# Moving kv times wo and the column sums one to three gate/up pairs later, and spacing the 16 divisions 2.75 pairs apart

## The chip, the cores and the metric

The kernel runs on one core of one Trainium2 chip. The metric is the device time of one execution in microseconds (us). The span of a profile, from the first to the last instruction, is 1.7 to 1.9 us shorter than the time of its run. PE is the matmul engine, PEld its weight loads (they overlap the matmuls), DVE the Vector engine, ACT the Scalar engine, POOL the GpSimd engine, SP the engine that issues most of the DMA transfers. PSUM is the memory, in banks, into which the matmuls write.

## The reference

One block over 2048 tokens of width 512: layer norm, then the sum of the input, a linear attention with 32 heads of 16, and a SwiGLU feed-forward of width 1792. In bfloat16, cut to what matters:

```python
xn = layernorm(x)
q, k, v = heads(xn @ wqkv)                  # 32 heads of 16
pq, pk = phi(q), phi(k)                     # phi(t) = where(t > 0, t + 1, exp(t)) + 1e-6
kv  = einsum("bhsd,bhse->bhde", pk, v)
z   = einsum("bhsd->bhd", pk)               # the column sums of phi(k)
num = einsum("bhqd,bhde->bhqe", pq, kv)
den = einsum("bhqd,bhd->bhq", pq, z)[..., None] + 1e-6
A   = (num / den) @ wo
B   = (silu(xn @ w_gate) * (xn @ w_up)) @ w_down
return x + A + B
```

## The kernel before

The first stage (up to 48.5 us) normalises, projects and accumulates phi(k) transposed times xn in four PSUM banks. The second stage is a loop over 56 gate/up pairs: 4 chunks of 512 tokens times 14 slices of the width 1792. One pair is 4 gate and 4 up matmuls on PE. The attention work is threaded through this loop, and from the second chunk on an output tile of 128 tokens is put in after 4 of every 14 pairs; the last four tiles follow the loop. The parts that the change and the argument touch:

```python
def add(...):  # every operation is put on its engine's list in program order;
    ...        # semaphores are derived from what it reads and writes

def gb(j):
    return 4 + 2 * (j % 2)              # two pairs of PSUM banks, so pair j+2 reuses those of pair j

def hop(j):                             # hT = silu(gate) * up, DVE
    C, fc = j // NFC, j % NFC
    K.add("dve", lambda e: e.tensor_tensor(out=hT[:, C % 2, fc, :],
        in0=banks[gb(j) + 1][:, :], in1=sil[:, j % 2, :], op=ALU.mult), ...)

def z_add(half, i):                     # a "token sum": zacc += phi(k) of one tile of 128 tokens
    acc, key = zacc[:, half, :], ("zacc", half)
    t = NZP * half + i                  # NZP = 10: tiles 0..9 on POOL, tiles 10..15 on DVE
    ...
    K.add("dve" if half else "pool", lambda e: e.tensor_tensor(out=acc, in0=first, in1=pk[:, t, :], op=ALU.add), ...)

def kv_mask(): ...                      # DVE: kvT = bank 0 times a block mask
def m_mm(g): ...                        # PE: M = kvT times wo; ACT copies it out
def z_bf(): ...                         # DVE: zb (bf16) = zacc[0] + zacc[1]
def z_mm(): ...                         # PE: ones times zb, the column sums; ACT copies them out to zbc
def pz_mul(t): ...                      # POOL: pz = phi(q) times zbc
def divide(t): ...                      # DVE: reduce pz per head, + 1e-6, reciprocal, pq *= 1/den
                                        # then a DMA transposes pq into pk (the tile of phi(q) that PE reads)

for j in range(NGU):                    # 56 pairs
    C, fc = j // NFC, j % NFC
    if j == 2:
        gu(j, kv_fns(), ...)            # 16 small kv matmuls between those of the pair
    else:
        gu(j)
    if j == 0:
        hop(j)
    elif j == 1:
        hop(j); z_add(1, 1); z_add(1, 2)
    elif j == 2:
        hop(j); kv_mask(); z_add(1, 3)
    elif j == 3:
        hop(j); z_add(1, 4); z_add(1, 5); m_mm(0); m_mm(1)
    elif j == 4:
        hop(j); z_bf(); m_mm(2); m_mm(3)
    elif j == 5:
        hop(j); z_mm()
    else:
        if j % 2 == 0 and j // 2 - 3 < NT:
            pz_mul(j // 2 - 3)
        hop(j)
        if j % 2 == 1 and j // 2 - 3 < NT:
            divide(j // 2 - 3)
    if C >= 1 and fc in O_SLOT:         # an output tile
        otile(4 * (C - 1) + O_SLOT[fc])
```

(Statements of one pair are put on one line here; cuts are marked with dots.)

## Time and profile before

| | before |
|---|---|
| time, median of the first 3 runs | 215.41 us (215.18 to 215.76) |
| span of the profile | 213.3 us |
| PE busy | 208.3 us, 98% |
| DVE busy | 126.4 us, 59% |
| first gate matmul to first output tile (PE timeline, 48.50 to 84.60) | 36.10 us |
| first output tile to the end of the last matmul (84.60 to 210.85) | 126.25 us |

The head of the page of before, with busy time, share of the span and instructions of each engine:

```profile
span 213.3 us, 2668 instructions
PE 208.3 (98%) x991; PEld 95.5 (45%) x991; DVE 126.4 (59%) x217; ACT 69.8 (33%) x138; POOL 55.5 (26%) x81
```

PE at 98% does not say that it runs at its peak, because a record of a matmul covers its pipeline as well: a record of 512 columns lasts 0.38 us here, while the next one can start after 0.216 us. The chain of waits (start, length, what) shows the pace. These are pieces of the chain of before, with engine, tile and line after start and length:

```profile
60.39 0.68 DVE hT L395
61.07 0.61 DVE zb L419
61.73 0.39 PE pb L423
62.12 22.64 PE pb L382 x104
84.76 0.86 PE pb L461 x4
85.62 3.02 PE pb L465 x14
88.64 5.18 PE pb L382 x24
```

The last line gives 5.18 / 24 = 0.216 us for a matmul of 512 columns, each with a weight load of its own. The piece at 62.12 is slower: 104 matmuls in 22.64 us, 0.2177 each, 0.19 us more than at 0.2158. And the chain runs through DVE until 61.73: PE waits there for zb, the bf16 sum. From the table of waits of before (who waited for whom: us in total, times, longest), the two lines of PE in this stage and three lines of the weight loads:

```profile
PE pb L423 <- DVE zb L419: 0.6, 1, 0.6
PE pb L455 <- DVE kvT L413: 0.2, 1, 0.2
...
PEld pb L382 <- DVE hT L395: 1.1, 3, 0.4
PEld pb L423 <- DVE zb L419: 1.1, 1, 1.1
PEld pb L455 <- DVE kvT L413: 0.7, 1, 0.7
```

L423 is the column-sum matmul, L455 kv times wo, L382 gate and up. These waits understate the loss, since a matmul's record reaches beyond the moment at which the next could start; the starts in PE's timeline against a pace of 0.2158 us are the better measure:

```profile
55.44 1.03 PE L382 MATMUL pb<-xnT,wu 128*128 128x512 bf16 x4
56.65 0.61 PE L455 MATMUL pb<-wo,kvT 128*128 128x512 bf16 x2 [0.18 <-DVE kvT L413]
...
60.11 1.03 PE L382 MATMUL pb<-xnT,wu 128*128 128x512 bf16 x4
61.73 0.39 PE L423 MATMUL pb<-zb,ones 128*128 128x512 bf16 x1 [0.59 <-DVE zb L419]
```

Four matmuls after 55.44 is 56.30, and kv times wo starts at 56.65; four after 60.11 is 60.97, and the column-sum matmul starts at 61.73. The DVE timeline of before (start, length) shows what DVE did at the time:

```profile
53.86 1.53 DVE L332 TENSOR_TENSOR zacc<-zacc,pk 128x512 f32<-128x512 f32 x1
55.31 0.68 DVE L395 TENSOR_TENSOR hT<-pb,sil 128x512 bf16<-128x512 f32 x1
55.91 0.68 DVE L413 TENSOR_TENSOR kvT<-pb,maskt 128x512 bf16<-128x512 f32 x1
56.51 1.67 DVE L332 TENSOR_TENSOR zacc<-zacc,pk 128x512 f32<-128x512 f32 x1
58.11 0.68 DVE L395 TENSOR_TENSOR hT<-pb,sil 128x512 bf16<-128x512 f32 x1
```

The second token sum stands ahead of the third hT product and of the mask on DVE's list, and it takes 1.53 us. A piece of work on an engine with a list delays all that follows it, even what PE wants sooner.

### The profile page before, as it was taken

To read this page: it belongs to the slowest core of one execution; us is meant where nothing else is said; L and a number is where in the kernel's file an instruction comes from. 1 tells how busy PE (TensorE), PEld (TensorE's weight loads), DVE (VectorE), ACT (ScalarE), POOL (GpSimd) and SP (SyncE) were. 2 spreads that over 40 slices of the span, in tenths; PEclk is the share of its full clock that TensorE was granted. 3 is DMA by queue.
4 is the path that set the end of the run, shared out by engine and by line. 5 is a ranking of instruction groups with operands and counts; after the bars stand their busy time and mean duration, and the time that the engine had idled before them with its cause. 6 is when DMAs were issued, how large, how long until landed. Compare 5 with 4: busy or idle time off the path is not lost.

```text
span 213.3 us, 2668 instructions
## 1 busy us (share of the span) xinstructions
PE 208.3 (98%) x991; PEld 95.5 (45%) x991; DVE 126.4 (59%) x217; ACT 69.8 (33%) x138; POOL 55.5 (26%) x81
## 2 busy tenths in 40 slices
PE   7999999999989999999999999999999999999995
PEld 2444444444434444444444444444444444444454
DVE  3899985546967999594677776663233223241121
ACT  3797975546553333122131313021123122130000
POOL 3257664559934332131222222000000000000000
DMA  6942332499900212112102020201000000000001
GB/s 193 352 104 49 71 67 58 129 379 375 353 21 0 52 25 49 47 27 52 25 25 49 26 52 25 49 25 49 3 25 0 25 0 29 0 25 23 26 28 49
DMA packets 26765, 15.78 MB, mean 74 GB/s; under 512 B 16512, under 2 KB 26752, under 8 KB 26752
## 3 DMA queue, kind: packets, MB, share of 16 engines
q1 hardware_dynamic: 25920, 14.88, 24.6%
q10 hardware_dynamic: 832, 0.72, 1.0%
q8 instruction: 8, 0.13, 0.3%
q14 instruction: 5, 0.04, 0.1%
HBM read 9.70 MB, written 2.10 MB: 55 GB/s over the span
## 4 chain that ended last, share of the span: by engine, by line
PE 89%; DVE 5%; ACT 2%; DMA 1%; issue 1%; SPq 0%; DVEq 0%
PE pb L382 41%; PE pb L465 23%; PE pb L295 13%; PE pb L319 6%; PE pb L461 6%; DVE zacc L332 2%; DVE hT L395 1%; DMA x_sb<-in_A_x_dram 1%; ACT L390 1%; ACT GT L402 1%; DVE stats L226 0%; DVE zb L419 0%; ACT sil L390 0%; ACT ef L303 0%; DVE kvT L413 0%
## 5 line engine op out<-in xcount | busy, mean ns | idle before, releaser
L390 ACT ACTIVATE sil<-pb 128x512 bf16<-128x512 f32 x56 | 33.3, 597 | 101.4 <-PE pb L382 100.1
L382 PE MATMUL pb<-xnT,wu 128*128 128x512 bf16 x224 | 57.8, 379 | 0.0
L382 PE MATMUL pb<-xnT,wg 128*128 128x512 bf16 x224 | 57.8, 379 | 0.0
L395 DVE TENSOR_TENSOR hT<-pb,sil 128x512 bf16<-128x512 f32 x56 | 37.6, 685 | 32.1 <-PE pb L382 30.4
L465 PE MATMUL pb<-wd,hT 128*128 128x512 bf16 (+1 forms) x238 | 51.2, 366 | 0.0
L465 PEld LDWEIGHTS pb<-wd,hT 128*128 128x128 bf16 x238 | 23.3, 98 | 25.1
L471 DVE TENSOR_TENSOR out_sb<-pb,x_sb 128x512 bf16<-128x512 f32 (+1 forms) x17 | 11.2, 660 | 37.7 <-PE pb L465 37.7
L382 PEld LDWEIGHTS pb<-xnT,wu 128*128 128x128 bf16 x224 | 21.7, 98 | 26.3 <-DVE hT L395 1.1
L382 PEld LDWEIGHTS pb<-xnT,wg 128*128 128x128 bf16 x224 | 21.9, 98 | 25.7
L432 POOL TENSOR_TENSOR pz<-pq,zbc 128x512 f32<-128x512 bf16 x16 | 18.5, 1161 | 55.0 <-DVE den L437 51.4
L295 PE MATMUL pb<-wqkv,xnT 128*128 128x512 bf16 x128 | 29.6, 379 | 0.1
L307 POOL TENSOR_SCALAR ef<-ef 128x512 bf16<-128x512 bf16 x32 | 19.4, 612 | 19.2 <-ACT ef L303 19.0
L303 ACT ACTIVATE ef<-pb 128x512 bf16<-128x512 f32 x32 | 18.3, 591 | 9.4 <-PE pb L295 9.2
L295 PEld LDWEIGHTS pb<-wqkv,xnT 128*128 128x128 bf16 x128 | 12.3, 98 | 15.1 <-ACT xnT L274 0.7
L444 DVE TENSOR_TENSOR pq<-pq,rden 128x512 bf16<-128x512 bf16 x16 | 17.5, 1091 | 0.6
L461 PE MATMUL pb<-M,pk 128*128 128x512 bf16 (+1 forms) x68 | 16.6, 366 | 0.0
L319 PE MATMUL pb<-pk,xn 128*128 128x512 bf16 x64 | 15.4, 379 | 0.0
L314 DVE SCALAR_TENSOR_TENSOR pk<-pb,ef 128x512 bf16<-128x512 f32 x16 | 10.8, 679 | 4.8 <-POOL ef L307 4.8
L314 DVE SCALAR_TENSOR_TENSOR pq<-pb,ef 128x512 bf16<-128x512 f32 x16 | 10.7, 682 | 3.9 <-POOL ef L307 3.9
L226 DVE BATCH_NORM_STATS2 stats<-x_sb 128x6 f32<-128x512 bf16 x16 | 10.9, 679 | 3.3 <-DMA x_sb<-in_A_x_dram 3.3
L437 DVE TENSOR_REDUCE den<-pz 128x32 f32<-128x512 f32 x16 | 10.8, 672 | 0.0
L332 POOL TENSOR_TENSOR zacc<-zacc,pk 128x512 f32<-128x512 f32 x8 | 10.2, 1277 | 0.6
(46 smaller groups left out, 78.1 us busy)
## 6 DMA issues: line engine op xcount, KB each, us to landing
out_dram<-out_sb SPq DMA_DIRECT2D x15, 128.0 KB, 1.7
x_sb<-in_A_x_dram SPq DMA_DIRECT2D x14, 128.0 KB, 4.2
wg<-in_B_w_gate_dram SPq DMA_DIRECT2D x2, 896.0 KB, 7.8
wu<-in_B_w_up_dram SPq DMA_DIRECT2D x2, 896.0 KB, 9.2
wd<-in_B_w_down_dram SPq DMA_DIRECT2D x2, 896.0 KB, 13.8
wqkv<-in_A_wqkv_dram ACTq DMA_DIRECT2D x2, 256.0 KB, 4.0
wqkv<-in_A_wqkv_dram SPq DMA_DIRECT2D x2, 256.0 KB, 4.6
wqkv<-in_A_wqkv_dram SPq DMA_DIRECT2D x1, 512.0 KB, 7.9
```

Of the source, the lines that this page charges most:

```text
L295: K.add("pe", [(lambda e, c=c: e.matmul(banks[b][:, :], xnT[:, c, t * P:(t + 1) * P], wqkv[:, c, col:col + D], start=(c == 0), stop=(c == ...
L303: K.add("act", lambda e: e.activation(ef[:, b - 4, :], banks[b][:, :], ACT.Exp), r=[B(b)], w=[("ef", b - 4)])
L307: K.add("pool", lambda e: e.tensor_scalar(out=buf, in0=buf, scalar1=1.0 + 1e-6, scalar2=0.0, op0=ALU.min, op1=ALU.max), r=[bkey], w=[bkey])
L314: K.add("dve", lambda e: e.scalar_tensor_tensor(out=dst, in0=banks[b][:, :], scalar=1e-6, in1=ef[:, b - 4, :], op0=ALU.max, op1=ALU.add), ...
L319: K.add("pe", [(lambda e, c=c: e.matmul(banks[c][:, :], xn[:, t, c * P:(c + 1) * P], pk[:, t, :], start=(t == 0), stop=(t == NT - 1))) for ...
L382: fns.append(lambda e, c=c, b=b, w_=w_: e.matmul(banks[b][:, :], w_[:, c, fc * P:(fc + 1) * P], xnT[:, c, C * 512:(C + 1) * 512], start=(c ...
L390: K.add("act", lambda e: e.activation(sil[:, j % 2, :], banks[gb(j)][:, :], ACT.Silu), r=[B(gb(j))], w=[("sil", j % 2)])
L395: K.add("dve", lambda e: e.tensor_tensor(out=hT[:, C % 2, fc, :], in0=banks[gb(j) + 1][:, :], in1=sil[:, j % 2, :], op=ALU.mult), r=[B(gb( ...
L432: K.add("pool", lambda e: e.tensor_tensor(out=pz[:, t % 2, :], in0=pq[:, t, :], in1=zbc[:, :], op=ALU.mult), r=[("pq", t), ("zbc",)], w=[( ...
L444: K.add("dve", lambda e: e.tensor_tensor(out=heads(pq[:, t, :]), in0=heads(pq[:, t, :]), in1=rden[:, i, :][:, :, None].broadcast_to([P, NH ...
L461: fns = [(lambda e, g=g: e.matmul(banks[bank][:, 0:hi - lo], pk[:, t, g * P:(g + 1) * P], M[:, g, lo:hi], start=(g == 0), stop=False)) for ...
L465: fns = [(lambda e, fc=fc: e.matmul(banks[bank][:, 0:hi - lo], hT[:, C % 2, fc, jj * P:(jj + 1) * P], wd[:, fc, lo:hi], start=False, stop= ...
```

## The change

The intent is to let PE run through without a wait: the mask moves ahead of the second token sum, DVE's five token sums are spread to one a pair (pairs 1 to 5, with the bf16 sum in pair 6), kv times wo is due one pair later, the column-sum matmul three pairs later, and the divisions start three pairs later and come every 2.75 pairs rather than every 2. No instruction is added or taken away.

```diff
+PZ_AT = {9 + 11 * t // 4: t for t in range(16)}
+DIV_AT = {j + 1: t for j, t in PZ_AT.items()}
...
-            if j == 0:
-                hop(j)
-            elif j == 1:
-                hop(j)
+            hop(j)
+            if j == 1:
                 z_add(1, 1)
+            elif j == 2:
+                kv_mask()
                 z_add(1, 2)
-            elif j == 2:
-                hop(j)
-                kv_mask()
+            elif j == 3:
                 z_add(1, 3)
-            elif j == 3:
-                hop(j)
-                z_add(1, 4)
-                z_add(1, 5)
+            elif j == 4:
                 m_mm(0)
                 m_mm(1)
-            elif j == 4:
-                hop(j)
-                z_bf()
+                z_add(1, 4)
+            elif j == 5:
                 m_mm(2)
                 m_mm(3)
-            elif j == 5:
-                hop(j)
+                z_add(1, 5)
+            elif j == 6:
+                z_bf()
+            elif j == 8:
                 z_mm()
-            else:
-                if j % 2 == 0 and j // 2 - 3 < NT:
-                    pz_mul(j // 2 - 3)
-                hop(j)
-                if j % 2 == 1 and j // 2 - 3 < NT:
-                    divide(j // 2 - 3)
+            if j in DIV_AT:
+                divide(DIV_AT[j])
+            if j in PZ_AT:
+                pz_mul(PZ_AT[j])
```

## The prediction

> What bounds the kernel now. The page's busy table has PE at 98% of a 213.3 us span, granted clock 1.000; the chain of waits is 89% PE. An unstalled run of 24 matmuls of 128x512 in the chain (5.18 us) gives 0.2158 us each; the Trainium skill, "TensorE: Matmul & The Clock Gate", section "Single matmul latency", states 215.7 ns for back-to-back 512-column matmuls, so this trace agrees. PE is therefore at its floor wherever the chain shows 0.216 us a matmul, and only gaps can be won.
>
> Gaps in the gate/up stage (timeline, PE):
> - From the first gate matmul (48.50) to the first one after the column-sum matmul (61.96): 13.46 us. The work is 48 gate/up matmuls, 4 kv-times-wo and 1 column-sum matmul at 0.2158, and 16 small kv matmuls costing about 0.056 each (the interleaved stretch repeats every 0.327 for one large and two small): 12.33 us. So 1.1 us is lost: 0.34 before the first kv-times-wo matmul (at 56.65 instead of 56.31, waiting for the masked kv, which DVE did only after two token sums), about 0.76 before the column-sum matmul (61.73 instead of 60.97, waiting for the bf16 sum on DVE, which also stands behind token sums). The table of waits shows 0.2 and 0.6 for these two.
> - 62.12 to 84.76: 104 matmuls take 22.64 us instead of 22.45. DVE does a division (0.67+0.18+0.35+1.15 us) and two hT products (1.27) in 3.58 us per two pairs, PE needs 3.45, so DVE slips 0.13 per division; the last three slips reach PE through bank reuse (weight loads waiting for hT). Loss 0.2 us.
> - From 84.76 to the end every chain piece is at 0.216: nothing to win.
>
> What the change does. It adds and removes no instruction's work; it reorders DVE and PE. Masking comes right after the third hT product (estimate: done at 56.2), and kv-times-wo is now due at 58.0: no wait. Each pair keeps one token sum on DVE (0.9 to 1.7 us, long while Pool sums too; the Trainium skill, "SBUF — State Buffer", section "SBUF: two separate sides", gives a port pair that Vector and Pool lock for a whole instruction; the trace agrees: the division's multiply takes 1.15 us beside Pool's multiply and 0.69 when Pool is idle). My hand schedule puts hT products 3 to 6 at least 0.8 us ahead of the matmuls that reuse their banks, and the bf16 sum at about 64.3, before the column-sum matmul at 65.8. Divisions every 2.75 pairs need about 2.35 + 2.75x0.65 = 4.1 us of DVE for 4.75 us of PE, so slips no longer add up. The divisions end at pair 51; each transpose (2.4 us) still lands at least five pairs before its output tile, except the last, which has about four tiles. So no new wait.
>
> Gain: 1.1 + 0.2 = 1.3 us, all on PE's path, nearly all realised.
>
> Predicted: 214.1 us, 8 in 10 within 213.7 to 214.8 (runs before scatter by 0.6). Faster by over 2%: 1%; within 2%: 98%; slower by over 2%: 1%.
>
> Right if: PE's waits for the masked kv and the bf16 sum vanish; 48.5 to the output tiles shows 0.216 per matmul; DVE-released weight-load idle disappears; span near 212.0. The multiplies of the division stay 1.15 us, as Pool still starts when the reduction frees its buffer. Wrong if token sums beside Pool stretch so that an hT product comes late for its bank (PE gaps at pairs 5 to 7), or if kernel time outside the trace's PE gaps moves.

## The result, and the profile after

The changed kernel took 213.81 us (median of 4 runs, 213.55 to 214.22), before 215.3 us (median of 4 runs). The ratio is 0.9925, with a 95% interval of 0.9909 to 0.9942. A ratio is the mean time of one kernel's fast runs over that of the other's of the same rounds, so it is not quite the ratio of the two medians; the plain means of the four and four runs give 0.9929.

The gain is 0.6 to 0.7%. The measured median lies inside the predicted range of 213.7 to 214.8, near its low end; the ratio applied to the median of before, 0.9925 x 215.3 = 213.7, lies on that end or just past it (213.68).

The head of the page of the changed kernel:

```profile
span 211.9 us, 2651 instructions
PE 207.5 (98%) x972; PEld 95.9 (45%) x991; DVE 125.3 (59%) x217; ACT 69.9 (33%) x138; POOL 55.7 (26%) x81
```

This trace lacks 19 matmul records (972 of 991, while the weight loads are all there); each lacking record leaves what looks like a short gap, so PE's busy time is not to be compared. The waits for zb and kvT are gone from the table of PE's waits of the changed kernel, which has a single line, a wait at the very start:

```profile
PE pb L218 <- PEq L570: 0.8, 1, 0.8
```

The weight loads waiting for hT are gone too. Pieces of the chain of the changed kernel, where from 8.62 us PE is the only engine until DVE's last addition at 209.56 (line numbers are 2 higher than before):

```profile
54.73 3.45 PE pb L384 x16
58.18 0.43 PE pb L457 x2
58.62 1.73 PE pb L384 x8
60.34 0.43 PE pb L457 x2
60.77 3.45 PE pb L384 x16
...
65.95 0.21 PE pb L425
66.17 8.85 PE pb L384 x41
75.02 0.05 issue
75.07 8.37 PE pb L384 x38
83.44 0.86 PE pb L463 x4
```

After the column sums (L425) the pace is 8.85 / 41 = 0.216 us; the "issue" of 0.05 us is the place of a lacking record.

DVE's timeline of the changed kernel shows the new order, the mask before the sum and one sum a pair:

```profile
54.84 0.69 DVE L397 TENSOR_TENSOR hT<-pb,sil 128x512 bf16<-128x512 f32 x1 [1.01 <-PE pb L409]
55.45 0.68 DVE L415 TENSOR_TENSOR kvT<-pb,maskt 128x512 bf16<-128x512 f32 x1
56.04 0.68 DVE L334 TENSOR_TENSOR zacc<-zacc,pk 128x512 f32<-128x512 f32 x1
56.64 0.68 DVE L397 TENSOR_TENSOR hT<-pb,sil 128x512 bf16<-128x512 f32 x1
57.24 1.05 DVE L334 TENSOR_TENSOR zacc<-zacc,pk 128x512 f32<-128x512 f32 x1
...
63.22 0.68 DVE L421 TENSOR_TENSOR zb<-zacc 128x512 bf16<-128x512 f32 x1
```

The mask ends at 56.13 and its first user starts at 58.02; the bf16 sum ends at 63.90 and its user starts at 65.79.

The marks on PE's timeline say where the time went. "Front" is the start of the first gate matmul, counted from the start of the span; "middle" runs from there to the first matmul of the first output tile; "rear" from there to the end of the last matmul.

| | front | middle | rear |
|---|---|---|---|
| before | 48.50 | 36.10 | 126.25 |
| changed | 48.49 | 34.78 | 126.26 |

The middle lost 1.32 us, the front and the rear nothing. The prediction's sum of gaps, from its own figures before rounding, was (13.46 - 12.33) + 0.19 = 1.32 us. And no gap is left in the middle: its 157 matmuls of 512 columns at 0.2158 us and 16 small ones at 0.056 us add to 34.78 us.

### The profile page after: what moved, and what is told of

The parts are those of the page before. It is cut to its first block, busy times and chain, and to the rows that moved or that the text cites. A ratio compares the mean times of both kernels' runs of the same rounds, so it can differ in the third digit from the quotient of the medians.

```text
span 211.9 us, 2651 instructions
## 1 busy us (share of the span) xinstructions
PE 207.5 (98%) x972; PEld 95.9 (45%) x991; DVE 125.3 (59%) x217; ACT 69.9 (33%) x138; POOL 55.7 (26%) x81
## 4 chain that ended last, share of the span: by engine, by line
PE 94%; DMA 3%; SPq 1%; issue 1%; DVE 0%
PE pb L384 45%; PE pb L467 23%; PE pb L297 12%; PE pb L321 7%; PE pb L463 7%; DMA wqkv<-in_A_wqkv_dram 3%; SPq L159 1%; PE pb L409 0%; PE pb L457 0%; DVE out_sb L473 0%; PE pb L425 0%
## 5 line engine op out<-in xcount | busy, mean ns | idle before, releaser
L384 PE MATMUL pb<-xnT,wg 128*128 128x512 bf16 x216 | 57.2, 379 | 0.4
```

Source lines behind the costliest of these rows:

```text
L384: fns.append(lambda e, c=c, b=b, w_=w_: e.matmul(banks[b][:, :], w_[:, c, fc * P:(fc + 1) * P], xnT[:, c, C * 512:(C + 1) * 512], start=(c ...
```

## The experiments

Ten further runs were made, all correct, three of them without an edit; the rounds of each were interleaved with runs of before on the same chip. Three questions were open: which part of the change brings how much, whether the gaps are independent of each other, and why the ratio is a little better than the gaps allow. The summary, with the marks of each kernel's profile (us) and the ratio to before:

| kernel | front | middle | rear | ratio (95% interval) |
|---|---|---|---|---|
| changed | 48.49 | 34.78 | 126.26 | 0.9925 (0.9909 to 0.9942) |
| after_again | 48.44 | 34.78 | 126.25 | 0.9938 (0.9920 to 0.9955) |
| after_third | 48.91 | 34.78 | 126.25 | 0.9946 (0.9933 to 0.9959) |
| before_again | 48.52 | 36.11 | 126.25 | 1.0000 (0.9985 to 1.0014) |
| div_only | 48.25 | 35.90 | 126.26 | 0.9979 (0.9967 to 0.9991) |
| early_only | 48.43 | 34.78 | 126.25 | 0.9939 (0.9926 to 0.9952) |
| mask_m_only | 48.38 | 36.20 | 126.25 | 0.9997 (0.9985 to 1.0010) |
| colsum_only | 48.61 | 35.15 | 126.25 | 0.9952 (0.9940 to 0.9965) |
| cadence_1p5 | 48.92 | 37.11 | 127.21 | 1.0098 (1.0084 to 1.0112) |
| sums_on_vector | 48.34 | 34.77 | 126.26 | 0.9942 (0.9930 to 0.9955) |
| colsum_pair7 | 48.99 | 34.78 | 126.25 | 0.9951 (0.9936 to 0.9966) |

### after_again: the size of the gain

No edit. What was expected:

> The changed kernel once more, to size the gain. Theory A (the gain is the PE gaps that the trace of before shows: 0.34 + 0.76 + 0.19 = 1.3 us): 1.3 us less than before, ratio 0.9940. Rival B (part of the gain lies outside the PE gaps, as the recorded ratio 0.9925 would be 1.6 us): ratio near 0.9925 again, and the traces' mark 'first output tile minus first gate matmul' shorter by clearly less than the time.

Measured: 213.75 us against 215.1 us, ratio 0.9938; the middle again 34.78 us. 1.32 us of 215.1 us would be 0.9939, so this comparison has the gain in the PE gaps and nothing beside them. Rival B is not supported, though the interval, 0.9920 to 0.9955, would hold 0.9925 too.

### div_only: the divisions alone

```diff
+PZ_AT = {6 + 11 * t // 4: t for t in range(16)}   # the early order stays as before
+DIV_AT = {j + 1: t for j, t in PZ_AT.items()}
```

> Only the divisions every 2.75 pairs, starting at pair 6 as before; the early order untouched. Theory A: only the slips of 0.2 us go (from the first column-sum matmul to the first output tile 104 matmuls at 0.216), both early waits (0.2 and 0.6 in the table of waits) stay; time 0.2 us less than before, ratio 0.999. Rival B (the cadence does more, because DVE and Pool collide less often): over 0.5 us less.

Measured: 214.75 us, ratio 0.9979 (0.9967 to 0.9991), which is 0.5 us (0.2 to 0.7), so that the ratio alone does not exclude rival B's 0.5 us; the middle went from 36.10 to 35.90 us. The 0.2 us of theory A is what the trace shows; both early waits stood unchanged at 0.2 and 0.6, and the stretch after the column sums now runs at 0.2159 us a matmul. In the chain of this kernel:

```profile
61.48 0.39 PE pb L425
61.87 22.45 PE pb L384 x104
```

The front of this profile was also 0.25 us shorter (48.25 instead of 48.50), ahead of all that the edit touches, which would account for the rest in this one run. The other four runs left no trace, so why the ratio is better than the marks allow stays open. The ratio alone would have put more than twice the effect on the divisions.

### early_only: the early order alone, divisions every 2 pairs from pair 9

```diff
-PZ_AT = {9 + 11 * t // 4: t for t in range(16)}   # of the changed kernel
+PZ_AT = {9 + 2 * t: t for t in range(16)}
```

> Only the early reorder; divisions every 2 pairs, starting three pairs later (pair 9). Theory A: 1.1 us less than before, ratio 0.995; no early PE wait; before the first output tile only 4 divisions fit, so the slip of 0.13 us each reaches 0.4 us and does not reach PE at all, in which case the whole 1.3 us comes without the wider spacing. Rival: the wider spacing is needed for 0.2 us or more.

Measured: 213.84 us, ratio 0.9939, middle 34.78 us: the whole gain, without the wider spacing. The stretch that lost 0.19 us before is at its pace in the chain of this kernel (17.27 / 80 = 0.2159):

```profile
65.89 0.21 PE pb L425
66.11 17.27 PE pb L384 x80
```

DVE still slips here: its reductions (the first step of a division) start at 70.28, 73.86, 77.44, 81.02 and 84.59 us, 3.58 us apart, where two pairs take PE 3.45. But the divisions start three pairs later, so that four of them, where there were six, start before the first output tile (at 83.21 us here, 84.60 before). During a tile PE asks for no new hT product for 3.9 us, and DVE catches up. One weight load still waits 0.3 us for an hT product, but no matmul does. So the 0.19 us can be had in two ways, by wider spacing (div_only) or by a later start (this kernel), and with the late start the wider spacing adds nothing.

### mask_m_only: the mask first and kv times wo a pair later, the column sums left

```diff
             elif j == 1:
-                z_add(1, 1); z_add(1, 2)
+                z_add(1, 1)
             elif j == 2:
-                kv_mask(); z_add(1, 3)
+                kv_mask(); z_add(1, 2); z_add(1, 3)
             elif j == 3:
-                z_add(1, 4); z_add(1, 5); m_mm(0); m_mm(1)
+                z_add(1, 4); z_add(1, 5)
             elif j == 4:
-                z_bf(); m_mm(2); m_mm(3)
+                m_mm(0); m_mm(1); z_bf()
             elif j == 5:
-                z_mm()
+                m_mm(2); m_mm(3); z_mm()
```

> Only the mask ahead of the second token sum and kv-times-wo one pair later; the column-sum matmul stays after pair 5 and divisions as before. Theory A1 (both waits hang on one DVE queue, the bf16 sum is ready when DVE has worked off its list, about 61.0 to 61.6 us): the wait for the masked kv goes, the wait for the bf16 sum stays or grows (0.5 to 1.1 us), so much of the 0.34 us is handed on; time 0 to 0.6 us less. Rival A2 (the two gaps are independent): the wait for the bf16 sum keeps its size of 0.76 us in PE's schedule and 0.34 us is gained.

Measured: 215.0 us, ratio 0.9997, middle 36.20 us (0.1 us more than before). PE's waits of this kernel:

```profile
PE pb L425 <- DVE zb L421: 1.1, 1, 1.1
PE pb L218 <- PEq L568: 0.8, 1, 0.8
```

The wait for kvT is gone, and the wait for zb has grown from 0.6 to 1.1 us. The column-sum matmul starts at 61.72 us, where it started at 61.73 before. This is theory A1: the 0.34 us were handed on in full, since the second wait ends when DVE has worked off its list, and that moment did not come sooner. (Counted from the first gate matmul it came 0.1 us later, 13.34 us instead of 13.23, which is the 0.1 us of the middle.) Rival A2 (0.34 us gained) falls.

### colsum_only: the bf16 sum and its matmul later, the mask left

```diff
+PZ_AT = {9 + 2 * t: t for t in range(16)}
...
             elif j == 4:
-                z_bf(); m_mm(2); m_mm(3)
-            elif j == 5:
+                m_mm(2); m_mm(3)
+            elif j == 6:
+                z_bf()
+            elif j == 8:
                 z_mm()
```

> Only the bf16 sum and the column-sum matmul moved later (after pairs 6 and 8), divisions every 2 pairs from pair 9; mask, token sums and kv-times-wo in the old places. Theory A (a gap goes only if the last wait behind the DVE list goes): the wait for the masked kv stays at 0.34 us of PE schedule, the 0.76 us and the 0.19 us of slips go; from the first gate matmul to the first output tile 35.12 us, ratio 0.9956. Rival (the kv wait matters for more than its 0.34): over 35.3 us.

Measured: 214.21 us, ratio 0.9952, middle 35.15 us against 35.12 expected. The only late wait left in PE's table is the one for kvT (0.2 us). So the move of the mask, with the spread token sums and kv times wo a pair later, is worth its 0.34 us (0.37 in the marks, from 35.15 here to 34.78 in early_only) only together with the later column sums, and the later column sums with the later start of the divisions are worth 0.95 us by themselves.

### cadence_1p5: more divisions per pair

```diff
-PZ_AT = {9 + 11 * t // 4: t for t in range(16)}
+PZ_AT = {9 + 3 * t // 2: t for t in range(16)}
```

> The changed kernel with a division every 1.5 pairs instead of 2.75. Theory A (DVE slips by the excess of 2.36 us a division plus 0.62 us an hT product over PE's 1.73 us a pair; PE feels it once the slip is over about 0.4 us): worked out with these durations, PE loses about 3.1 us against the changed kernel, all in weight loads waiting for hT; ratio to before 1.008. Rival (spacing of divisions is of no account): ratio 0.994.

Measured: 217.32 us, ratio 1.0098; the middle grew by 2.33 us and the rear by 0.95 us against the changed kernel, together 3.3 us (expected 3.1). In time it is 3.5 us against the 213.86 us of the changed kernel, and the ratio lies above the 1.008 that was expected, which its interval (1.0084 to 1.0112) leaves just outside. The waits of this kernel are for the engine that theory A names, though not in weight loads alone:

```profile
PE pb L384 <- DVE hT L397: 2.6, 3, 1.1
...
PEld pb L384 <- DVE hT L397: 4.6, 4, 1.6
```

So the slip adds up as told: while a division and its share of hT products take DVE longer than the pairs take PE, the excess is stored up, and it reaches PE after some slack, through the two pairs of PSUM banks.

### sums_on_vector: no token sums on POOL

```diff
-        NZP = 10                            # token sums of tiles 0..9 on POOL
+        NZP = 0                             # all on DVE: tile 15 is added in z_bf,
+                                            # sums put after pairs 0 to 9, z_mm after pair 11
-PZ_AT = {9 + 11 * t // 4: t for t in range(16)}
+PZ_AT = {12 + 11 * t // 4: t for t in range(16)}
```

> The changed kernel with all 15 token sums on DVE, none on Pool; column-sum matmul after pair 11, divisions every 2.75 pairs from pair 13. Theory L (a token sum on DVE is stretched by waiting for Pool's sum to end): with Pool idle every sum of DVE takes 0.69 us, none over 0.75, and as PE is never late the time is that of the changed kernel, ratio 0.994. Rival (the stretch is DVE's own, or due to the weight loads then in flight): sums still range from 0.7 to 1.7 us.

Measured: 213.85 us, ratio 0.9942, middle 34.77 us. The token sums on DVE by line and form (min/median/max in ns), first of before, then of this kernel:

```profile
L332 DVE TENSOR_TENSOR zacc<-zacc,pk x4: 693/1284/1671, 53.9 to 59.8; 128x512 f32<-128x512 f32 x4
```

```profile
L334 DVE TENSOR_TENSOR zacc<-zacc,pk x13: 681/682/693, 53.4 to 68.2; 128x512 f32<-128x512 f32 x13
```

With POOL idle every sum takes 0.68 to 0.69 us: the stretch to 1.67 us came from POOL. The Trainium skill, "SBUF — State Buffer", section "SBUF: two separate sides", says that a DVE instruction with two SBUF inputs contends with a GpSimd instruction that reads SBUF and that the loser waits for the whole instruction. This run agrees, and so does the trace of before: every token sum and every multiply of DVE that started while an instruction of POOL ran ended 0.55 us after that instruction's end (DVE's sum of 53.86 at 55.39, POOL's at 54.84). The division's multiply, two SBUF inputs as well, still has a median of 1.15 us in all kernels, since POOL's next multiply is released by the reduction just before it; the last two, for which POOL has none left, take 0.69 us. And though DVE's list here carries 15 sums, no matmul of the second stage waits: what counts is not the sum of DVE's work but what stands ahead of an item that PE needs.

One question stays open. In the kernel before, the five sums of DVE took 5.82 us, 2.4 us more than at 0.68 us each (an estimate from these durations), which is more than the 1.13 us that PE lost early. So the old order might have cost PE little if POOL had been out of the way; no run kept the old order without POOL's sums.

### before_again and after_third: how far a comparison strays

No edit in either: the kernel before against itself, and the changed kernel a third time.

> The kernel before against itself, to see how far a comparison of equal kernels strays. Expected ratio 1.000, with an interval of about 0.0015 either way; PE marks (first gate matmul to first output tile 36.10 us) equal to 0.02 us. If equal kernels stray by 0.001 or more, the step from 0.9925 (on record) to 0.9938 (changed kernel again) is scatter of the comparison and not a second effect of the change. Rival: equal kernels agree to 0.0003, and 0.9925 wants another cause.

> The changed kernel a third time. Recorded ratios so far 0.9925 and 0.9938, while the PE marks of the traces differ from before by 1.32 us in both, which alone would be 0.9939. Theory A (0.9925 was scatter): ratio 0.9932 to 0.9945, PE mark from first gate matmul to first output tile 34.78 us. Rival B (a further 0.3 us outside the marks): ratio 0.992 to 0.993.

Measured: before against itself 1.0000 (0.9985 to 1.0014), middle 36.11 us; the changed kernel 0.9946 (0.9933 to 0.9959), middle 34.78 us, for the third time. The equal kernels did not stray by the 0.001 that I had set as a sign of scatter; taken by its letter, that run went to the rival (they agreed to 0.0003), and it did not settle the question. The third comparison of the changed kernel did: with the same marks it came out a hair above the 0.9932 to 0.9945 that theory A gave, and away from the 0.992 to 0.993 of rival B. The three ratios for one kernel are 0.9925, 0.9938 and 0.9946. The first comparison's runs of before had a mean of 215.39 us (4 runs), those of the later comparisons 215.15 us (31 runs); the changed kernel had 213.85 us there and 213.86 us over all its 15 runs. So the surplus of the ratio on record sat in the runs of before. The mean of all 41 runs of before, with the six of before_again, is 215.18 us, and the 15 of the changed kernel differ from it by 1.32 us.

Part of the run-to-run scatter can be seen in the traces. The front of the changed kernel was 48.44 us in after_again and 48.91 us in after_third, 0.47 us apart. The chain of waits of after_again, then of after_third, where the first weights arrive:

```profile
2.71 5.80 DMA wqkv<-in_A_wqkv_dram
```

```profile
2.70 6.28 DMA wqkv<-in_A_wqkv_dram
```

These weights took 0.48 us longer in the second profile, and PE's whole schedule stood 0.47 us later from there. This is the same work in both kernels, ahead of all that the change touches. Why the four first runs of before were slower cannot be read, as only one of them left a trace. The three later calls ran on three chips, so a difference between chips is not excluded.

### colsum_pair7: how much of the shift is to spare

```diff
-PZ_AT = {9 + 11 * t // 4: t for t in range(16)}
+PZ_AT = {8 + 11 * t // 4: t for t in range(16)}
...
-            elif j == 8:
+            elif j == 7:
                 z_mm()
```

> The changed kernel with the column-sum matmul after pair 7 instead of 8, divisions one pair earlier. In the changed kernel the bf16 sum ends on DVE at 63.90 us, and pair 7 ends on PE at 64.06. Theory A (only the moment the sum is ready against PE's schedule counts): no wait, PE mark still 34.78 us, ratio 0.994; so one pair of the shift is to spare. Rival (a sum so close to its use costs PE a wait): a wait of 0.1 to 0.3 us for the bf16 sum and a mark of 34.9 to 35.1 us.

Measured: 214.12 us, ratio 0.9951 (3 rounds; 0.9936 to 0.9966), middle 34.78 us; PE has no wait for zb in its table, only its weight load one of 0.2 us, which no matmul felt. (The record of the column-sum matmul itself is one of those that this trace lacks.) The ratio is worse than the 0.9939 of the marks, though its interval holds it; the front of the profiled run was 48.99 us, and of the other three runs no trace tells. So, by the marks, two pairs of delay would do where the change uses three.

## Why the prediction was right or wrong

- **What bounds the kernel: right.** PE has the chain, at 0.216 us a matmul, and only gaps could be won.
- **The sizes of the gaps: right.** 1.13 us early and 0.19 us of slips were read from the trace of before; the middle shortened by 1.32 us in every profile of the changed kernel.
- **No new wait: right.** The schedule worked out by hand put the mask at 56.2 us (56.13 measured), the bf16 sum at 64.3 us (63.90) and the column-sum matmul at 65.8 us (65.79).
- **"The multiplies of the division stay 1.15 us": right** (median 1.148 us after).
- **The time of before, and the range laid round it: this is the step that failed.** The predicted 214.1 us is a sum of two terms, a before of 215.41 us less 1.3 us. The second held (1.32 us). The first, the median of three runs, was too high: the mean of all 41 runs of before is 215.18 us, and 215.18 - 1.32 is the 213.86 us that the 15 runs of the changed kernel took. So the forecast stood 0.2 us too high, and its low end of 213.7 us left only 0.4 us below for the scatter of a comparison, although the text itself had noted that the runs of before scatter by 0.6 us. A comparison of four runs with four had an interval of 0.0016 to 0.0017, about 0.35 us, either way; the one on record came out at 1.6 us (0.0075 x 215.3), 0.3 us more than the gaps. The two later comparisons gave 1.3 us (0.0062 x 215.1) and 1.2 us (0.0054 x 215.07). The mis-sized term is thus the time of before with its margin, 0.23 us in 215.41, and not one of the gaps, whose sum the runs confirmed: no second effect of the change showed in three traces with equal marks.
- **"Divisions every 2.75 pairs ... so slips no longer add up": true, but credited to the wrong part; here a step of the mechanism failed, at no cost to the number.** The prediction booked the 0.2 us to the wider spacing. early_only has it all with a division every 2 pairs, because of the later start. The wider spacing is sufficient alone (div_only), but not needed in the changed kernel.
- **The gaps as a sum: right for the whole change, and misleading for its parts.** 0.34 and 0.76 us were written down as two terms. mask_m_only shows that the first is worth nothing while the second stays, since both hang on one list on DVE.
- **Token sums of "0.9 to 1.7 us": too long.** They took 0.68 to 1.05 us after, and the last of them ran after POOL had finished its own. It cost nothing, as it was an error on the safe side.

## What to carry to other kernels

Where one engine is at its pace in all but a few places, sum the gaps in its timeline against that pace, and work out for each waited-for item what stands ahead of it on its producer's list; that sum is the most that a reorder of this stretch can give at the same pace, and here it came true to 0.02 us in the marks. Gaps that hang on one list are not separate terms: take away the last first, since taking away an earlier one alone hands its wait on (here all of its 0.34 us). For an effect below one per cent compare the marks of the traces and give the predicted time the scatter of a whole comparison, both kernels' runs included.

## What the Trainium skill lacked or had wrong

- "TensorE: Matmul & The Clock Gate", section "Back-to-back issue gap", gives a sustained pace in a stream of weight load and matmul pairs of about 131 ns for 512 columns, and says that 216 ns over-counts. Here every 512-column matmul has its own weight load, the streams are long (24 in 5.18 us, 80 in 17.27 us), and the pace is 0.216 us. The figure of the section "Wait — 56ns, not 53.3ns?" (215.7 ns back to back, warm) is the one that these traces show.
- The same section gives about 81 ns for 128 columns in such a stream. In the kv stretch, one 512-column matmul and two 128-column ones repeat every 0.327 us, which leaves about 0.056 us for each small one (in a mixed stream; no run has a stream of small ones alone).
- "SBUF — State Buffer", section "Who interferes with whom", tells of the lock between Vector and GpSimd, but it does not say how the wait looks in a profile: it is inside the instruction's own duration (a sum of 0.68 us is recorded with up to 1.67 us, a multiply of 0.69 us with 1.15 us), not in the idle time before it, and in the trace of before each such instruction ends 0.55 us after POOL's does.
- No page that I read gives the run-to-run scatter of a kernel of this length: runs of the unchanged kernel lay between 214.7 and 215.8 us, and the arrival of the first weights alone moved by 0.48 us between two profiles of one kernel.
